# Attention and token mixing on one NeuronCore: output tiles of two batches stored whole, three stores on other queues

## The chip, the core and the metric

The kernel runs on one NeuronCore of a Trainium2 chip. The core has five engines that run side by side, each with its own instruction stream in order: TensorE (PE, matrix products, results into the eight banks of PSUM), VectorE (DVE), ScalarE (ACT), GpSimd (POOL) and SyncE (SP, which here only issues DMAs). DMAs are issued by SyncE, ScalarE or GpSimd, each into its own queue, and carried out by 16 DMA engines that all queues share. Engines wait for each other, and for DMAs that have landed, through semaphores. The metric is device time in microseconds (us) of the whole program.

## The reference

Inputs are fp32: q, k, v of shape (8 batches, 8 heads, 576, 64), p of shape (8, 8, 32, 64), w_q and w_k of 512 x 64 and w_out of 512 x 512. The output is fp32, (8, 576, 512): 9.4 MB.

```python
def _attn_ref(q, k, v, p):
    scale = 1.0 / np.sqrt(q.shape[-1])
    def sm_attn(qq, kk, vv):
        s = scale * np.matmul(qq, kk.transpose(0, 1, 3, 2))
        s = s - np.max(s, axis=-1, keepdims=True)
        a = np.exp(s)
        a = a / (np.sum(a, axis=-1, keepdims=True) + 1e-09)
        return np.matmul(a, vv)
    p_packed = sm_attn(p, k, v)
    return sm_attn(q, p_packed, p_packed)

def _moe_ref(x, w_q, w_k, w_out):     # x: heads side by side, (8, 576, 512)
    wq = x @ w_q
    wk = x @ w_k
    W_tok = scale * np.einsum('bsd,btd->bst', wq, wk)
    mixed = np.einsum('bst,btd->bsd', W_tok, x)
    return np.maximum(mixed, 0.0) @ w_out
```

## The kernel before

The whole program is a list of steps written out by hand, the string ORDER. Each entry is a step with its batch, a part, the engine (`@A` ScalarE, `@V` VectorE, `@P` GpSimd; for a store, none means SyncE) and the PSUM banks (`=0,1`). The loop at the end (L601 to L622) issues the entries in this order, so on every engine, and in every DMA queue, work stands in the order of the string. Semaphore waits are put in where a step reads or overwrites what another step or DMA uses.

For each batch the steps run in this order: loads of k, v and q (LD, all by GpSimd, which casts them to bf16); the first attention (KT, S1, X1, TE, PV, RC, PP, PT); the second attention (QK, QKE, QV, S2, X2, RS, RR, AM, AT, AE); the token mixing with its products WKQ (evacuated by WE), GM (GE), Y (YE), MX and MR (RL, RLF, RLR); and the output products OT with w_out, whose results are copied from PSUM to an fp32 tile in SBUF (OE for two of its four tiles, OEF for one, OEH for a part of one). The batches overlap; the last, batch 7, runs alone at the end.

What the change and the prediction speak of:

- The output of a batch is 4 tiles of 128 x 512 in the buffer `o`, plus a rest of 64 rows that two batches share (`orem`, OEF.b.4). There are NO = 6 `o` buffers of 8 KB per partition, so batch 6 uses the buffer of batch 0 and batch 7 that of batch 1. The partition holds tokens so that its 4 tiles are one run of 8 KB in the output.
- `ST.b.n` (L555) stores tiles 2n and 2n+1 of batch b, 128 rows of 4 KB, 512 KB; `ST.b.4` stores the rest of two batches, 256 KB. `STF.b.t` (L590) stores one tile, 256 KB, and `STH` (L585) a part of batch 7's last one.
- `HOLD.v7` (L567) is a tiny DMA by SyncE that reads the last of v; SyncE issues it once that has landed, and all SyncE's stores stand behind it.
- `OEF.6.2@A` and `OEF.6.3@V` write tiles 2 and 3 of batch 6, `OE.6.0@V` its tiles 0 and 1. `WE.7.0@A` and `WE.7.1@A` copy what `GM.7` multiplies, and stand behind OEF.6.2 on ScalarE. On TensorE, OT.6.0 and OT.6.1 stand between WKQ.7 and GM.7.
- `AM` (L405) is GpSimd's own arithmetic; AM.6.2 is the next after its early stores.

Line 128 is the copy by ScalarE, 132 by VectorE, 441 and 446 the products of WKQ, 467 those of GM, 540 and 578 those of the output.

Of the kernel before, what the change touches and what calls it, by code (L numbers as in the profile page):

```python
# [40 lines left out]
S1.6=4,5,6,7 X1.6.0@A GM.4=0 GE.4@V TE.6.0@V LD.r7 OT.3.1 X1.6.1@A TE.6.1@V Y.4=0,1 OE.3.0@A RS.5.4@V RR.5.4@V  # L41
PV.6.0=4,5 YE.4@A PV.6.1 MX.4.0=6,7 RC.6@V RL.4.0@A PP.6.0@V AM.5.3@P PP.6.1@V PT.6@V MX.4.1=2,3 AM.5.2@P
OT.3.2=0,1 OT.3.3 RL.4.1@A QK.6=4 QKE.6@A QV.6.2@V ST.2.1 S2.6.2=6,7 X2.6.2@A S2.6.3=2,3 ST.3.4 MR.4=4,5
X2.6.3@A OE.3.1@V RLR.4@V KT.7.2@V AT.5.2=6 AE.5.2@A AT.5.3=7 OT.4.0=0,1 OT.4.1 AE.5.3@A WKQ.5.0=4,5 WKQ.5.2
OE.4.0@A ST.1.1@P WKQ.5.1 RS.6.4@V WE.5.2@A RR.6.4@V ST.4.0 ST.0.1@P S1.7=2,3,6,7 X1.7.1@A AM.6.3@V ST.3.0@P
OT.4.2=0,1 GM.5=4 TE.7.1@V OT.4.3 AT.6.3=5 X1.7.0@A TE.7.0@V GE.5@A OE.4.1@A AM.6.2@P AT.6.2=4 ST.2.0 Y.5=6,7
YE.5@A ST.0.0 ST.3.1 PV.7.0=2,3 QV.7.1@V AE.6.3@V QV.7.0@V AE.6.2@A QD.6@P PV.7.1 RC.7@V PP.7.0@V PP.7.1@V
PT.7@V MR.5=0,1 RLR.5@A MX.5.1=6,7 RL.5.1@A MX.5.0=4,5 RL.5.0@V WKQ.6.0=0,1 WKQ.6.1 WKQ.6.2 WE.6.2@A OT.5.4=2
OEF.5.4@A S2.7.1=6,7 ST.5.4 ST.1.0 GM.6=3 GE.6@V X2.7.1@A RS.7.1@V RR.7.1@V S2.7.2=0,1 X2.7.2@A S2.7.0=4,5
QK.7=2 X2.7.0@A RS.7.0@V RR.7.0@V Y.6=6,7 YE.6@A OT.5.2=0,1 MX.6.1=4,5 QKE.7@A MX.6.0=6,7 AM.7.1@P RS.7.2@V  # L50
RR.7.2@V MR.6=2,3 OT.5.3 RLR.6@V RL.6.0@V RL.6.1@A OE.5.1@A ST.4.1 AM.7.0@P OT.5.0=2,3 AM.7.2@P AT.7.0=4
AE.7.0@A AT.7.1=5 AE.7.1@V AT.7.2=6 AE.7.2@V OT.6.2=0,1 OEF.6.2@A QD.7@P WKQ.7.0=4,5 WKQ.7.2 WKQ.7.1 WE.7.0@A
WE.7.1@A STF.6.2 OT.6.0=6,7 OT.6.1 GM.7=0 OE.6.0@V OT.5.1 OE.5.0@V ST.5.1@P GE.7@A Y.7=4,5 OT.6.3 OEF.6.3@V
ST.6.0 STF.6.3 YE.7@A ST.5.0 MR.7=6,7 RLR.7@A MX.7.0=4,5 RLF.7.0.1@A RLF.7.0.0@V MX.7.1=2,3 RLF.7.1.0@A
OT.7.4=0 OEF.7.4@A ST.7.4 RLF.7.1.1@V OT.7.1=6 OEF.7.1@V OT.7.0=7 STF.7.1 OT.7.2=1 OEF.7.0@A OH.7.0=0 STF.7.0
OEF.7.2@A STF.7.2 OEH.7.0@V STH.7.0 OH.7.1=5 OEH.7.1@A STH.7.1@A
"""


# [1 line left out]
def kernel(  # L61
# [27 lines left out]
    P = 128  # L89
# [47 lines left out]
    def halves(x):  # L137
        return slice(x * 64, (x + 1) * 64)
# [79 lines left out]
    T = {}  # L218
# [323 lines left out]
    def orows(b):  # L542
        return out[b].rearrange("(g r) n -> g r n", r=R)[:, 0:8].rearrange("g (y t) n -> g y (t n)", y=2)
# [11 lines left out]
    def ST(b, n, eng, bk):  # L555
        q = {"A": nc.scalar, "P": nc.gpsimd}.get(eng, nc.sync)
        if n == 4:
            dst = out.rearrange("b (g r) n -> (b g) r n", r=R)
            q.dma_start(dst[(b - 1) * GR:(b + 1) * GR, R - 1], T["orem", b // 2])
        elif b in TURN:  # L560
            q.dma_start(orows(b)[:, :, n * 2 * D:(n + 1) * 2 * D],
                        T["o", b][:, 2 * n:2 * n + 2].rearrange("a t n -> a (t n)"))
        else:
            q.dma_start(orows(b)[:, n], T["o", b][halves(n)].rearrange("a t n -> a (t n)"))
# [25 lines left out]
    def STF(b, t, eng, bk):  # L590
# [4 lines left out]
                 PT=PT, QK=QK, QKE=QKE, QD=QD, QV=QV, S2=S2, X2=X2, HA=HA, RS=RS, RR=RR, AM=AM,  # L595
                 AT=AT, AE=AE, WKQ=WKQ, WE=WE, GM=GM, GE=GE, Y=Y, YE=YE, MX=MX, MR=MR, RL=RL, RLF=RLF,
                 RLR=RLR, OT=OT, OE=OE, OEF=OEF, ST=ST, STF=STF,
                 OH=OH, OEH=OEH, STH=STH)

    with tc.manual_schedule():  # L600
        for item in ORDER.split():  # L601
# [9 lines left out]
            elif f[0] == "WARM":  # L611
                n = 128 * int(f[1])
# [38 lines left out]
```

## Time and profile before

| | us |
|---|---|
| median of 3 runs | 104.38 (104.2 to 105.15) |
| the profiled execution | 104.42 |
| its span, first to last instruction | 102.6 |

Below, each digit stands for a fortieth of the span (2.57 us): the share of time that GpSimd was busy, that the 16 DMA engines were busy on the mean, in tenths, and the GB/s that they moved. Loads run to slice 30, stores from there on.

```profile
POOL 5971877993039929724459493649724009300000
...
DMA  1999999999999999999999999999999999997893
GB/s 18 234 230 207 211 215 209 207 210 213 203 212 207 214 209 209 213 210 207 212 210 208 211 212 204 216 211 205 250 250 387 412 413 409 417 388 294 346 370 127
```

The stores as the page counts them (engine whose queue, number, KB of each, median us from issue to landing):

```profile
out_dram<-o SPq DMA_DIRECT2D x9, 512.0 KB, 8.9
...
out_dram<-o POOLq DMA_DIRECT2D x4, 512.0 KB, 9.0
out_dram<-o SPq DMA_DIRECT2D x5, 256.0 KB, 3.0
...
out_dram<-orem SPq DMA_DIRECT2D x3, 256.0 KB, 7.8
```

GpSimd issues ST.1.1, ST.0.1 and ST.3.0 one behind the other after its arithmetic for batch 5, and ST.5.1 near the end. SyncE's order is ST.2.1, ST.3.4, ST.4.0, ST.2.0, ST.0.0, ST.3.1, ST.5.4, ST.1.0, ST.4.1, STF.6.2, ST.6.0, STF.6.3, ST.5.0 and then batch 7. In the views a store by `ST` has line 561 (559 for a rest), one by `STF` line 592, one by `STH` line 588.

### The profile page before, as it was taken

The numbers are of one execution on the slowest core, as the hardware profiler recorded it, in microseconds if no ns is written. First come the engines' busy times: TensorE is split into PE (matmuls) and PEld (weight loads), VectorE is DVE, ScalarE is ACT, GpSimd is POOL, SyncE is SP. The second block draws the span as 40 slices with busy tenths as digits, with TensorE's granted clock in tenths as the row PEclk, the third lists the DMA queues.
The fourth block names the chain that finished last, engine by engine and source line by source line (L and its number), as shares of the span: only waits on it lengthen the run. The fifth ranks groups of instructions, "written<-read, shape, count | busy, mean of one in ns | idle before, by whom it ended". The sixth has DMA issues, their size and how long they took to land.

```text
span 102.6 us, 3594 instructions
## 1 busy us (share of the span) xinstructions
PE 93.2 (91%) x1536; PEld 55.1 (54%) x1536; DVE 73.5 (72%) x140; ACT 65.0 (63%) x111; POOL 53.1 (52%) x83
## 2 busy tenths in 40 slices
PE   5998999998699999999998899989999999999930
PEld 3896555465265633755636557544757565643420
DVE  4164376957979479888697979499999979249420
ACT  1320415178754767849977979887989897726430
POOL 5971877993039929724459493649724009300000
PEclk9999999999999999999999999999999999999997
DMA  1999999999999999999999999999999999997893
GB/s 18 234 230 207 211 215 209 207 210 213 203 212 207 214 209 209 213 210 207 212 210 208 211 212 204 216 211 205 250 250 387 412 413 409 417 388 294 346 370 127
DMA packets 13567, 25.13 MB, mean 245 GB/s; under 512 B 1072, under 2 KB 6448, under 8 KB 13552
## 3 DMA queue, kind: packets, MB, share of 16 engines
q0 software_dynamic: 9936, 17.04, 84.3%
q1 hardware_dynamic: 3056, 7.41, 18.9%
q10 hardware_dynamic: 560, 0.46, 1.9%
q8 instruction: 12, 0.20, 0.7%
q14 instruction: 3, 0.02, 0.1%
HBM read 30.15 MB, written 9.44 MB: 386 GB/s over the span
## 4 chain that ended last, share of the span: by engine, by line
PE 64%; DVE 9%; ACT 8%; DMA 7%; POOL 4%; issue 3%; DVEq 0%; POOLq 0%; ACTq 0%
PE ps L540 26%; PE ps L617 9%; DMA k_sb<-in_k_dram 7%; PE ps L373 5%; PE ps L315 4%; ACT e1T L293 4%; POOL a L405 4%; PE ps L282 3%; PE ps L419 3%; PE ps L446 3%; PE ps L467 3%; DVE rs L394 2%; PE ps L441 2%; PE ps L336 2%; DVE kT L237 2%
## 5 line engine op out<-in xcount | busy, mean ns | idle before, releaser
L540 PE MATMUL ps<-wout,relu 128*128 128x512 bf16 x124 | 30.6, 380 | 0.0
L405 POOL TENSOR_TENSOR a<-e,rr 128x256 bf16<-128x256 f32 (+2 forms) x18 | 19.5, 1099 | 16.4 <-DVE rr L399 6.4
L617 PE MATMUL ps<-o 128*128 128x128 f32 (+3 forms) x76 | 20.0, 410 | 1.2 <-DVE o L135 1.2
L540 PEld LDWEIGHTS <-relu 128*128 128x128 bf16 x124 | 10.7, 98 | 11.7 <-issue 1.1
L128 ACT ACTIVATE o<-ps 128x1024 f32<-128x1024 f32 (+2 forms) x13 | 11.3, 870 | 5.4 <-PE ps L540 5.2
L617 PEld LDWEIGHTS ps<-o 128*128 128x128 f32 x76 | 11.8, 217 | 5.2 <-issue 3.6
L503 ACT ACTIVATE relu<-ps 128x1024 bf16<-128x1024 f32 (+1 forms) x14 | 12.9, 966 | 1.1 <-PE ps L492 1.1
L293 ACT ACTIVATE e1T<-ps 128x576 bf16<-128x576 f32 x16 | 9.8, 655 | 5.2 <-PE ps L282 4.6
L378 ACT ACTIVATE e<-ps 128x256 f32<-128x256 f32 (+2 forms) x19 | 11.2, 622 | 2.5 <-PE ps L373 2.4
L394 DVE TENSOR_REDUCE rs<-e 128x16 f32<-128x512 f32 (+2 forms) x13 | 10.9, 841 | 2.3 <-ACT e L378 2.2
L173 POOL DMA_DIRECT2D v_sb<-in_v_dram x16 | 10.0, 629 | 4.2 <-DMA v_sb<-in_v_dram 1.6
L237 DVE STREAM_TRANSPOSE kT<-k_sb 128x1152 uint32<-128x1152 uint32 (+1 forms) x9 | 11.0, 1226 | 1.4 <-DMA k_sb<-in_k_dram 1.3
L237 DVE STREAM_TRANSPOSE qT<-q_sb 128x1152 uint32<-128x1152 uint32 (+1 forms) x10 | 11.0, 1104 | 0.0
L132 DVE COPY o<-ps 128x1024 f32<-128x1024 f32 (+2 forms) x7 | 6.7, 977 | 5.2 <-PE ps L540 2.7
L237 DVE STREAM_TRANSPOSE e<-e1T 128x288 uint32<-128x288 uint32 x16 | 7.4, 468 | 3.1 <-ACT e1T L293 2.6
L128 ACT ACTIVATE aT<-ps 128x128 bf16<-128x128 f32 (+2 forms) x11 | 5.0, 464 | 5.7 <-PE ps L419 3.3
L128 ACT ACTIVATE wkq<-ps 128x448 bf16<-128x448 f32 (+1 forms) x10 | 7.2, 729 | 1.8 <-PE ps L446 1.7
L315 PE MATMUL ps<-v_sb,e 64*64 64x192 bf16 x288 | 7.5, 245 | 0.8 <-DVE e L237 0.5
L315 PEld LDWEIGHTS <-e 64*64 64x64 bf16 x288 | 5.9, 107 | 2.6 <-DVE e L237 2.0
L373 PEld LDWEIGHTS <-qT 64*128 64x128 bf16 x320 | 5.4, 94 | 2.6 <-DVE qT L237 1.5
L446 PE MATMUL ps<-aT,pqk 128*128 128x256 bf16 (+1 forms) x48 | 6.8, 246 | 0.0
L373 PE MATMUL ps<-ppT,qT 64*128 64x64 bf16 x320 | 6.6, 190 | 0.1
(70 smaller groups left out, 131.5 us busy)
## 6 DMA issues: line engine op xcount, KB each, us to landing
v_sb<-in_v_dram POOLq DMA_DIRECT2D x16, 288.0 KB, 14.5
out_dram<-o SPq DMA_DIRECT2D x9, 512.0 KB, 8.9
k_sb<-in_k_dram POOLq DMA_DIRECT2D x7, 576.0 KB, 14.0
q_sb<-in_q_dram POOLq DMA_DIRECT2D x6, 576.0 KB, 13.5
out_dram<-o POOLq DMA_DIRECT2D x4, 512.0 KB, 9.0
out_dram<-o SPq DMA_DIRECT2D x5, 256.0 KB, 3.0
q_sb<-in_q_dram POOLq DMA_DIRECT2D x4, 288.0 KB, 10.5
out_dram<-orem SPq DMA_DIRECT2D x3, 256.0 KB, 7.8
```

Of the source, the lines that this page charges most:

```text
L128: nc.scalar.activation(o, i, COPY)
L173: nc.gpsimd.dma_start(v_bufs[b % NL][halves(i), 0:7:2], src)
L237: nc.vector.transpose(o, i)
L293: nc.scalar.activation(e1T[:, x], T["s1", b][x].rearrange("a c m -> a m c"), EXP, scale=scale)
L315: nc.tensor.matmul(T["pv", b][halves(cc), i], lhsT, rhs, start=n == 0, stop=n == R - 1, skip_group_check=True)
L373: nc.tensor.matmul(ps[:, y, t - t0, i], lhsT, rhs, start=e == 0, stop=e == 1)
L378: nc.scalar.activation(e2[:, t0:t1].rearrange("a t (i y n) -> a y (t i) n", i=2, y=2), T["s2", b, c].rearrange("a y t i n -> a y (t i) n") ...
L394: nc.vector.tensor_reduce(rs[:, t0 * H:t1 * H], src, axis=AX, op=ADD)
L405: e.tensor_tensor(a2[:, t0:t1].rearrange("a t i (u l) -> a (t i u) l", l=L), e2v(b, c), T["rr", b][:, t0 * H:t1 * H].to_broadcast((P, (t1 ...
L503: nc.scalar.activation(o, i, RELU)
L540: nc.tensor.matmul(ps, lhsT, wout[:, j, :], start=j == 0, stop=j == NJ - 1)
L617: nc.tensor.matmul(bank(int(bk), [w]), warm[:, 0:P], rhs, start=True, stop=True)
```

## The change

ST gets a part 8, the whole tile buffer of a batch in one DMA with rows of 8 KB:

```diff
         if n == 4:
             dst = out.rearrange("b (g r) n -> (b g) r n", r=R)
             q.dma_start(dst[(b - 1) * GR:(b + 1) * GR, R - 1], T["orem", b // 2])
+        elif n == 8:
+            q.dma_start(orows(b), T["o", b].rearrange("a t n -> a (t n)"))
         elif b in TURN:
```

In ORDER these entries move (the others keep their places):

```diff
-X2.6.3@A OE.3.1@V RLR.4@V KT.7.2@V AT.5.2=6
+X2.6.3@A OE.3.1@V RLR.4@V ST.1.8@P KT.7.2@V AT.5.2=6
...
-OE.4.0@A ST.1.1@P WKQ.5.1 RS.6.4@V WE.5.2@A RR.6.4@V ST.4.0 ST.0.1@P S1.7=2,3,6,7 X1.7.1@A AM.6.3@V ST.3.0@P
+OE.4.0@A WKQ.5.1 RS.6.4@V WE.5.2@A RR.6.4@V ST.4.0 ST.3.8@P S1.7=2,3,6,7 X1.7.1@A AM.6.3@V
...
-YE.5@A ST.0.0 ST.3.1 PV.7.0=2,3
+YE.5@A ST.0.0 ST.0.1 PV.7.0=2,3
...
-OEF.5.4@A S2.7.1=6,7 ST.5.4 ST.1.0 GM.6=3
+OEF.5.4@A S2.7.1=6,7 ST.5.4 GM.6=3
...
-OT.5.1 OE.5.0@V ST.5.1@P GE.7@A
+OT.5.1 OE.5.0@V ST.5.1 GE.7@A
```

So GpSimd issues ST.1.8 and ST.3.8, of 1 MB each, in the place of ST.1.1, ST.0.1 and ST.3.0, and no store after them. SyncE's order becomes ST.2.1, ST.3.4, ST.4.0, ST.2.0, ST.0.0, ST.0.1, ST.5.4, ST.4.1, STF.6.2, ST.5.1, ST.6.0, STF.6.3, ST.5.0 and then batch 7.

More of the change, by code (lines that the diff above doesn't have):

```diff
@@ L43 @@
 OT.3.2=0,1 OT.3.3 RL.4.1@A QK.6=4 QKE.6@A QV.6.2@V ST.2.1 S2.6.2=6,7 X2.6.2@A S2.6.3=2,3 ST.3.4 MR.4=4,5
-X2.6.3@A OE.3.1@V RLR.4@V KT.7.2@V AT.5.2=6 AE.5.2@A AT.5.3=7 OT.4.0=0,1 OT.4.1 AE.5.3@A WKQ.5.0=4,5 WKQ.5.2
-OE.4.0@A ST.1.1@P WKQ.5.1 RS.6.4@V WE.5.2@A RR.6.4@V ST.4.0 ST.0.1@P S1.7=2,3,6,7 X1.7.1@A AM.6.3@V ST.3.0@P
-OT.4.2=0,1 GM.5=4 TE.7.1@V OT.4.3 AT.6.3=5 X1.7.0@A TE.7.0@V GE.5@A OE.4.1@A AM.6.2@P AT.6.2=4 ST.2.0 Y.5=6,7
-YE.5@A ST.0.0 ST.3.1 PV.7.0=2,3 QV.7.1@V AE.6.3@V QV.7.0@V AE.6.2@A QD.6@P PV.7.1 RC.7@V PP.7.0@V PP.7.1@V
@@ L48 @@
[L48 to L56, printed above, removed]
+X2.6.3@A OE.3.1@V RLR.4@V ST.1.8@P KT.7.2@V AT.5.2=6 AE.5.2@A AT.5.3=7 OT.4.0=0,1 OT.4.1 AE.5.3@A WKQ.5.0=4,5
@@ new lines @@
+WKQ.5.2 OE.4.0@A WKQ.5.1 RS.6.4@V WE.5.2@A RR.6.4@V ST.4.0 ST.3.8@P S1.7=2,3,6,7 X1.7.1@A AM.6.3@V OT.4.2=0,1
+GM.5=4 TE.7.1@V OT.4.3 AT.6.3=5 X1.7.0@A TE.7.0@V GE.5@A OE.4.1@A AM.6.2@P AT.6.2=4 ST.2.0 Y.5=6,7 YE.5@A
+ST.0.0 ST.0.1 PV.7.0=2,3 QV.7.1@V AE.6.3@V QV.7.0@V AE.6.2@A QD.6@P PV.7.1 RC.7@V PP.7.0@V PP.7.1@V PT.7@V
+MR.5=0,1 RLR.5@A MX.5.1=6,7 RL.5.1@A MX.5.0=4,5 RL.5.0@V WKQ.6.0=0,1 WKQ.6.1 WKQ.6.2 WE.6.2@A OT.5.4=2
+OEF.5.4@A S2.7.1=6,7 ST.5.4 GM.6=3 GE.6@V X2.7.1@A RS.7.1@V RR.7.1@V S2.7.2=0,1 X2.7.2@A S2.7.0=4,5 QK.7=2
@@ new lines @@
+X2.7.0@A RS.7.0@V RR.7.0@V Y.6=6,7 YE.6@A OT.5.2=0,1 MX.6.1=4,5 QKE.7@A MX.6.0=6,7 AM.7.1@P RS.7.2@V RR.7.2@V
+MR.6=2,3 OT.5.3 RLR.6@V RL.6.0@V RL.6.1@A OE.5.1@A ST.4.1 AM.7.0@P OT.5.0=2,3 AM.7.2@P AT.7.0=4 AE.7.0@A
+AT.7.1=5 AE.7.1@V AT.7.2=6 AE.7.2@V OT.6.2=0,1 OEF.6.2@A QD.7@P WKQ.7.0=4,5 WKQ.7.2 WKQ.7.1 WE.7.0@A WE.7.1@A
+STF.6.2 OT.6.0=6,7 OT.6.1 GM.7=0 OE.6.0@V OT.5.1 OE.5.0@V ST.5.1 GE.7@A Y.7=4,5 OT.6.3 OEF.6.3@V ST.6.0
+STF.6.3 YE.7@A ST.5.0 MR.7=6,7 RLR.7@A MX.7.0=4,5 RLF.7.0.1@A RLF.7.0.0@V MX.7.1=2,3 RLF.7.1.0@A OT.7.4=0
@@ L57 @@
+OEF.7.4@A ST.7.4 RLF.7.1.1@V OT.7.1=6 OEF.7.1@V OT.7.0=7 STF.7.1 OT.7.2=1 OEF.7.0@A OH.7.0=0 STF.7.0 OEF.7.2@A
+STF.7.2 OEH.7.0@V STH.7.0 OH.7.1=5 OEH.7.1@A STH.7.1@A
 """
```

## The prediction

> **What bounds the kernel now.** I read the page's shares first, then the chain of waits over the last 18 us.
>
> ```profile
> PE 93.2 (91%) x1536; PEld 55.1 (54%) x1536; DVE 73.5 (72%) x140; ACT 65.0 (63%) x111; POOL 53.1 (52%) x83
> ```
> ```profile
> 88.57 0.12 PE ps L441 x4
> ...
> 89.35 1.73 PE ps L540 x8
> 91.08 0.29 PE ps L467 x10
> 91.37 0.86 PE ps L540 x4
> ...
> 94.03 3.63 PE ps L540 x16
> 97.66 0.67 PE ps L578 x4
> ...
> 98.40 0.56 DVE o L132
> ```
>
> The columns are start, length and what ran. TensorE (PE) has hardly a gap: L441 is the last projection of batch 7 (WKQ.7), L540 and L578 are the products with w_out, and L467 is GM.7, from which all the rest of batch 7 follows in one line. After the copy OEH.7.0 at 98.40 only the last stores are left. So a change here costs time if it moves GM.7 and gains only if it shortens that line.
>
> Stores are on no link of that chain, but they are near it. A store matters in one way before the end: until it has landed, the o buffer that it reads can't be written again. There are 6 buffers for 8 batches, so batch 6 writes into batch 0's buffer and batch 7 into batch 1's. These are the first steps of ScalarE that do so, from its timeline:
>
> ```profile
> 88.60 0.60 ACT L128 ACTIVATE o<-ps 128x512 f32<-128x512 f32 x1 [0.55 <-PE ps L540]
> 89.10 0.97 ACT L128 ACTIVATE wkq<-ps 128x448 bf16<-128x448 f32 x2
> 91.41 0.28 ACT L128 ACTIVATE g<-ps 128x128 bf16<-128x128 f32 x1 [1.34 <-PE ps L467]
> ```
>
> The row at 88.60 is OEF.6.2@A, which writes tile 2 of o buffer 0, the tile that ST.0.1 reads. The row behind it is WE.7.0@A and WE.7.1@A, the operands of GM.7. Now ST.0.1 is GpSimd's second store; start and issue-to-landing (last column) are:
>
> ```profile
> 72.51 0.62 POOL L561 DMA_DIRECT2D out_dram<-o  x1
> out_dram<-o POOLq DMA_DIRECT2D x1, 512.0 KB, 9.7
> ```
>
> It lands at 72.51 + 9.7 = 82.2, which is 6.4 us ahead of OEF.6.2. The wait exists and is hidden.
>
> **The change part by part.**
>
> *ST.0.1 moves to SyncE, behind ST.0.0.* That is the sixth store of SyncE's queue, the place that ST.3.1 had. From SyncE's timeline and the issues, for ST.0.0 and then ST.3.1:
>
> ```profile
> 78.68 1.21 SPq L561 DMA_DIRECT2D out_dram<-o  x1
> out_dram<-o SPq DMA_DIRECT2D x1, 512.0 KB, 10.4
> 79.94 0.60 SPq L561 DMA_DIRECT2D out_dram<-o  x1
> out_dram<-o SPq DMA_DIRECT2D x1, 512.0 KB, 10.4
> ```
>
> They landed at 89.1 and 90.3. So even with nothing else changed, ST.0.1 in that place would land 1.7 us after OEF.6.2 wants its tile. (The wait goes by tiles and not by the whole buffer: OEF.6.2 began at 88.60, before ST.0.0, which reads tiles 0 and 1, had landed.)
>
> *GpSimd stores batches 1 and 3 whole.* Its early stores grow from three of 512 KB to two of 1 MB: from 1.5 to 2.0 MB. Whether the extra 512 KB lies ahead of ST.0.1 is read from the DMA queues (q0 is GpSimd's, q1 SyncE's; packets, MB, share of 16 engines) at 76 to 80, 80 to 84 and 84 to 88 us:
>
> ```profile
> q0 software_dynamic: 428, 1.40, 101.5%
> q1 hardware_dynamic: 50, 0.02, 2.1%
> ...
> q1 hardware_dynamic: 423, 1.30, 81.2%
> q0 software_dynamic: 111, 0.36, 22.4%
> ...
> q1 hardware_dynamic: 478, 1.62, 100.6%
> ```
>
> GpSimd's stores were issued first; its queue is emptied first and is gone by 84, six us before ST.3.1 landed, and SyncE's queue hardly moves until 80. With 0.52 MB more it would be gone by about 85.3, still long before ST.0.1's bytes. The engines are full (100.6%) and move 1.62 MB in 4 us, 0.405 MB per us. So 0.524 MB ahead costs 1.3 us, and the two SyncE stores above, 1.2 us apart in landing, say the same. ST.0.1 lands at 90.3 + 1.3 = 91.6, and ST.0.0 at 89.1 + 1.3 = 90.4.
>
> *The row length.* A row of 8 KB is in no store of this trace. Below: the 2 KB rows that fill the queue at 95.5 to 96 us take more time per byte than the 4 KB rows above:
>
> ```profile
> q1 hardware_dynamic: 92, 0.19, 102.3%
> ```
>
> That is 0.19 MB in 8.2 us of engine time, 23.2 KB per us, against 1.62 MB in 64.4 us, 25.2 KB per us. If doubling the row again gave as much again (8%), the 2.1 MB of GpSimd would take 0.4 us less of their 5.2 us. Above: the largest packets of the page, the instruction queue's,
>
> ```profile
> q8 instruction: 12, 0.20, 0.7%
> ```
>
> run at 0.20 MB in 0.7% of 16 x 102.6 us, 17 KB per us; at that rate the two stores would take 2.4 us more. They are reads of another kind, and the nearest row is the 4 KB store, so I take no difference.
>
> A fixed cost per DMA, of which one fewer now stands ahead of ST.0.1, isn't seen between them: the two 512 KB stores above landed 1.2 us apart, which their bytes alone take. The Trainium skill (DMA: Bandwidth & Descriptors, Anatomy of one DMA — SWDGE (gpsimd) path) gives a DMA some 2 us beside its bytes and asks for DMAs of 1 MiB; paid one after the other, that would make the sum 2 us less here (B below), and this trace disagrees by the 1.2 us.
>
> *What the wait costs.* OEF.6.2 goes from 88.60 to 91.6: 3.0 us later. Queued behind it on ScalarE are WE.7.0 and WE.7.1 (their end goes from 89.10 + 0.97 = 90.07 to 93.07), then GE.7, YE.7 and the rest of batch 7; on SyncE STF.6.2 waits for the same tile, and with it ST.5.1, ST.6.0 and all later stores. On TensorE the eight products OT.6.0 and OT.6.1 stand between WKQ.7 and GM.7 (89.35 to 91.08) and need neither; they cover 91.08 - 90.07 = 1.0 us. The rest, 3.0 - 1.0 = 2.0 us, is idle time of TensorE before GM.7, whose work is in a fixed order, so nothing moves into the gap. Small corrections cancel: four of GM.7's ten products need only WE.7.0 (0.1 us earlier), and the signal of the landing has to reach ScalarE (0.1 us later).
>
> After GM.7 the line is dependent to its end and moves by the same 2.0 us. One thing can give some back. VectorE's copies
>
> ```profile
> 91.12 3.05 DVE L132 COPY o<-ps 128x1024 f32<-128x1024 f32 x3 [2.74 <-PE ps L540]
> 94.08 1.28 DVE L505 TENSOR_SCALAR relu<-ps 128x512 bf16<-128x512 f32 x2
> ```
>
> stand packed in front of two of the four RLF.7 steps; the first (OE.6.0) stays at about 91.1, as ST.0.0 lands at 90.4, and the others move. The sixteen products at 94.03 take 3.63 us, 0.23 each, where eight at 89.35 take 0.216 each, so at most 0.2 us comes back. I count nothing.
>
> *The rest has one answer.* ST.1.0 and ST.3.1 leave SyncE, and ST.5.1 comes from GpSimd. No later step writes batch 3's or 5's buffer, and ST.1.8, now first on GpSimd, lands long before OEF.7.1 writes batch 1's. On GpSimd the rows are:
>
> ```profile
> 71.56 1.23 DVE L132 COPY o<-ps 128x1024 f32<-128x1024 f32 x1
> 71.84 1.89 POOL L561 DMA_DIRECT2D out_dram<-o  x3
> 76.36 1.58 POOL L405 TENSOR_TENSOR a<-e,rr 128x256 bf16<-128x256 f32 x1 [2.63 <-DVE rr L399]
> ```
>
> ST.3.8 now needs OE.3.1@V (the first row), over at 72.79, 0.3 us after GpSimd reaches it; it delays only itself, since GpSimd is idle 2.63 us before AM.6.2. Two issues instead of three, at 0.63 each or up to twice that for twice the bytes, fit in the same cover (2.5 us at most against 1.89); without it 0.6 us would be on AM.6.2. STF.6.2 and ST.6.0 on SyncE:
>
> ```profile
> 89.23 0.54 SPq L592 DMA_DIRECT2D out_dram<-o  x1
> 92.37 0.54 SPq L561 DMA_DIRECT2D out_dram<-o  x1
> ```
>
> Issuing ST.5.1 between them costs SyncE another 0.54 us; in the new order STF.6.2 goes out at about 92.2 and ST.6.0 at 93.3, and nobody waits for either.
>
> At the end, SyncE's stores from STF.6.2 on are 3.4 MB (ST.5.1 with them), 8.4 us at 0.405 MB per us. Issued from 92.2, with their first bytes some 1.5 us later, they end near 102.1. The last one, issued at 98.99 now and with this row,
>
> ```profile
> 98.99 0.54 SPq L588 DMA_DIRECT2D out_dram<-o  x1
> out_dram<-o SPq DMA_DIRECT2D x1, 192.0 KB, 2.5
> ```
>
> would be issued at 101.0 and land at 103.5, so it isn't held up by a backlog.
>
> Sum: 3.0 - 1.0 = +2.0 us. The profiled execution took 104.42 us with a span of 102.6 (1.8 us around it); the median of the three times is 104.38, within 0.04. So 106.4 us.
>
> **The rivals.**
>
> *A. Not slower: the 512 KB more on GpSimd's queue delay nothing on SyncE's.* The place is the landing of ST.0.1. If the engines served SyncE's queue beside GpSimd's, as in 80 to 84 us where q1 has 81% and q0 22%, or gained 0.4 us by longer rows, the landing would stay near 90.3. Then OEF.6.2 is 1.7 us late, 1.0 of it covered: 104.4 + 0.7 = 105.1 us. It decides from a landing at 90.6: earlier, the loss is under 1.04 us, which is 1%, about what a measurement of this kernel can tell from no change. Against it: the queue's emptying by 84 whatever the share in between.
>
> *B. The merging itself pays.* The last store, 192 KB, took 2.5 us to land, of which its bytes at 0.405 MB per us are 0.5: 2.0 us belong to no byte. If GpSimd's queue paid them between its stores, two in place of three would land ST.0.1 at 91.6 - 2.0 = 89.6; the cover of 1.0 us takes the rest, and the time is 104.4 us. Against it stand the two landings 1.2 us apart.
>
> *C. The idle time costs clock.* TensorE's granted clock after its last product (OH.7.1, over by 98.53), over the two stretches 98.53 to 101.14 and 101.20 to the end:
>
> ```profile
> 98.53:101.14 2.61, 0.00 (x0) 0.00 (x0) 0.43 (x1) 0.28 (x1) 0.00 (x0) 1.00 0.94 339
> 101.20:102.60 1.40, 0.00 (x0) 0.00 (x0) 0.00 (x0) 0.00 (x0) 0.00 (x0) 0.50 0.01 2
> ```
>
> After 2.6 us without work the clock (third number from the end) is halved. The new gap, from 91.08 to 93.1, is 0.6 us shorter than that, so I expect full clock. If the gap grows or is counted otherwise, the products behind it run at half clock. How long isn't shown: between the 1.4 us seen above and all of the 7.2 us left (91.08 to 98.32); midway, some 4 us, of which half is lost, gives 106.4 + 2 = 108.4. The Trainium skill (TensorE: Matmul & The Clock Gate, Part 1: The HAM clock gate) puts the gate's free-running window at 3.4 us, by which a gap of 2.0 us doesn't close it; the row here, closed after 2.6 us, shows that less than 3.4 us after the last product can be enough.
>
> *D. Rows of 8 KB go at 17 KB per us*: landing 2.4 us later, 108.8.
>
> **How the numbers follow.** Forecast, 106.4 (105.6 to 107.2 by its own terms, some 0.8 us on the landing): 0.70. A: 0.12. B: 0.05. C: 0.09. D: 0.04. The range goes from 104.9, which takes in A, to 107.9, a landing 1.5 us later than worked out, and leaves out B, C and D, together 0.18. Slower by over 1% (above 105.4): the forecast, C and D, 0.83. Within 1%: A and most of B, 0.14. Faster by over 1%: 0.03, a rest of B, since no link of the chain gets shorter.
>
> **What would show it.** Right: ST.0.1 lands near 91.6; OEF.6.2 begins then, and the idle time before it is ended by a DMA of out_dram; TensorE shows one new gap of about 2 us before L467; from there each row is shifted alike; OE.6.0 stays at 91.1; the clock stays at 1.00 until the last product. Wrong: OEF.6.2 at 88.6, a landing before 90, AM.6.2 late behind GpSimd's issues, last stores taking well over 2.5 us, or a gap at another place.

## The result and the profile after

| | before | after |
|---|---|---|
| median, us | 104.38 (104.12 to 105.15, 5 runs) | 106.25 (105.83 to 106.47, 5 runs) |
| ratio after to before | | 1.016, 95% interval 1.0132 to 1.0187 |
| profiled execution, us (span) | 104.42 (102.6) | 106.47 (104.7) |

The changed kernel is 1.9 us slower; 106.4 was forecast. In its code line 561 is the whole store, 563 an `ST` with rows of 4 KB, 594 an `STF`, 590 an `STH`. ScalarE's timeline in the changed kernel, at the place that the prediction named:

```profile
87.67 0.60 ACT L128 ACTIVATE aT<-ps 128x512 bf16<-128x512 bf16 x1
91.25 0.60 ACT L128 ACTIVATE o<-ps 128x512 f32<-128x512 f32 x1 [2.98 <-DMA out_dram<-o]
91.74 0.97 ACT L128 ACTIVATE wkq<-ps 128x448 bf16<-128x448 f32 x2
```

The first row is the copy that stands in front of OEF.6.2 (the aT copy). OEF.6.2 begins at 91.25 instead of 88.60, after 2.98 us in which ScalarE did nothing and which a store ended. Of these, 0.55 us were there before, for the products that OEF.6.2 copies; the store adds some 2.4. ST.0.1, in the views of SyncE's timeline and of the issues, is

```profile
79.86 0.60 SPq L563 DMA_DIRECT2D out_dram<-o  x1
out_dram<-o SPq DMA_DIRECT2D x1, 512.0 KB, 11.3
```

issued at 79.86 and landed at 91.2. TensorE's timeline shows the gap that comes of it, between the last output products in front of GM.7 and GM.7 itself (L467), with 0.16 us more between its first four products and the other six, as each part waits for its own WE.7:

```profile
89.40 1.89 PE L540 MATMUL ps<-wout,relu 128*128 128x512 bf16 x7
92.33 0.28 PE L467 MATMUL ps<-wkq,a 128*128 128x64 bf16 x4 [1.04 <-ACT wkq L128]
92.77 0.34 PE L467 MATMUL ps<-wkq,a 128*128 128x64 bf16 x6 [0.16 <-ACT wkq L128]
```

The chain of waits runs through the store now, and after GM.7 through the same links as before:

```profile
79.86 11.30 DMA out_dram<-o
...
91.25 0.07 ACT o L128
...
91.74 0.98 ACT wkq L128 x2
...
92.77 0.34 PE ps L467 x6
93.10 0.86 PE ps L540 x4
...
100.14 0.56 DVE o L132
```

The six products end at 93.10 where GM.7 ended at 91.37: 1.73 us later. The last copy starts at 100.14 where it started at 98.40: 1.74 us later. So nothing is lost or regained in between. Some 0.2 us of it is no part of the wait, as the aT copy above stood at 87.46 before; that leaves 1.5. What remains stands behind it, in the last store:

```profile
out_dram<-o SPq DMA_DIRECT2D x1, 192.0 KB, 3.0
```

It took 3.0 us where it took 2.5. Before, ScalarE's store landed last, 0.2 us behind SyncE's, so only 0.3 of these 0.5 us make the program longer: 0.2 + 1.5 + 0.3 is 2.0, of the 2.05 us between the two profiled executions.

### The profile page after: what moved, and what is told of

Same layout as the page of the kernel before. It is cut to its first block, busy times and chain, and to the rows that moved or that the text cites. A ratio compares the mean times of both kernels' runs of the same rounds, so it can differ in the third digit from the quotient of the medians.

```text
span 104.7 us, 3575 instructions
## 1 busy us (share of the span) xinstructions
PE 92.9 (89%) x1521; PEld 55.9 (53%) x1536; DVE 73.7 (70%) x140; ACT 65.0 (62%) x111; POOL 52.0 (50%) x81
## 4 chain that ended last, share of the span: by engine, by line
PE 54%; DVE 11%; DMA 11%; ACT 11%; issue 5%; POOL 4%; DVEq 0%; ACTq 0%; POOLq 0%
PE ps L619 17%; PE ps L540 17%; DMA out_dram<-o 11%; ACT e1T L293 5%; PE ps L373 4%; POOL a L405 4%; PE ps L315 3%; PE ps L419 2%; DVE rs L394 2%; DVE e L237 2%; PE ps L282 2%; ACT wkq L128 2%; PE ps L336 2%; PE ps L446 1%; PE ps L467 1%
## 5 line engine op out<-in xcount | busy, mean ns | idle before, releaser
L540 PE MATMUL ps<-wout,relu 128*128 128x512 bf16 x112 | 29.5, 380 | 0.9 <-issue 0.3
L619 PE MATMUL ps<-o 128*128 128x128 f32 (+3 forms) x76 | 20.8, 426 | 1.2 <-DVE o L135 1.2
L619 PEld LDWEIGHTS ps<-o 128*128 128x128 f32 x76 | 12.7, 233 | 5.3 <-issue 3.6
L446 PE MATMUL ps<-aT,pqk 128*128 128x256 bf16 (+1 forms) x48 | 6.8, 246 | 0.0
## 6 DMA issues: line engine op xcount, KB each, us to landing
q_sb<-in_q_dram POOLq DMA_DIRECT2D x4, 288.0 KB, 10.3
```

The source lines that it names most:

```text
L540: nc.tensor.matmul(ps, lhsT, wout[:, j, :], start=j == 0, stop=j == NJ - 1)
L619: nc.tensor.matmul(bank(int(bk), [w]), warm[:, 0:P], rhs, start=True, stop=True)
```

## The experiments

Two theories were put against each other. The wait theory: the loss is OEF.6.2 waiting for ST.0.1's landing. The rival: the loss is DMA work itself (rows of 8 KB, more bytes on GpSimd's queue, ST.5.1 among the last stores), and would be there without the wait. The table gives the median, the 95% interval of the ratio to the kernel before, run on the same chip, and four readings of each profiled execution: where ST.0.1 landed (issue plus the time to landing), where OEF.6.2 and GM.7 began (us), and how long SyncE's last store took. Executions differ by some tenths of a us from the start; that of e2 is the slowest of its kernel (105.36), and the steps read here come about 1.2 us late in it. The diffs show the entries around what moves, without the rest of their lines.

| | median us | ratio | ST.0.1 landed | OEF.6.2 | GM.7 | last store |
|---|---|---|---|---|---|---|
| before | 104.38 | | 82.2 | 88.60 | 90.92 | 2.5 |
| changed | 106.25 | 1.0132 to 1.0187 | 91.2 | 91.25 | 92.33 | 3.0 |
| e1_swap_only | 104.68 | 0.9987 to 1.0023 | 89.9 | 89.96 | 91.45 | 2.5 |
| e2_first | 104.53 | 0.9979 to 1.0021 | 85.8 | 89.76 | 92.08 | 2.5 |
| e3_rows4k | 106.59 | 1.0166 to 1.0228 | 91.5 | 91.58 | 92.66 | 3.1 |
| e4_other_buffer | 104.44 | 0.9975 to 1.0026 | 91.2 | 88.48 | 90.79 | 2.5 |
| e5_st51_pool | 105.90 | 1.0107 to 1.0172 | 91.2 | 91.24 | 92.32 | 2.5 |
| e6_later | 109.20 | 1.0419 to 1.0493 | 93.3 | 93.36 | 94.44 | 2.5 |
| e7_batch0_whole | 104.42 | 0.9987 to 1.0026 | 85.6 | 88.85 | 91.16 | 2.5 |
| e8_fifth | 105.16 | 1.0047 to 1.0115 | 89.8 | 89.87 | 91.23 | 3.0 |
| e9_fifth_st51_pool | 104.78 | 1.0005 to 1.0047 | 89.7 | 89.79 | 91.26 | 2.5 |
| e10_st51_ahead | 105.65 | 1.0097 to 1.0148 | 90.9 | 91.00 | 92.08 | 2.5 |
| e11_changed_again | 106.38 | 1.0158 to 1.021 | 91.1 | 91.15 | 92.36 | 2.9 |

**The wait alone taken away (e4_other_buffer).** Batch 6 writes into batch 2's buffer; no DMA changes.

```diff
-        T[key, b] = T[key][b % bufs]
+        T[key, b] = T[key][2 if (key, b) == ("o", 6) else b % bufs]
```

> The changed kernel with batch 6's output in the buffer of batch 2 instead of batch 0; every DMA in its place, size and queue as changed. Wait theory: OEF.6.2 now needs ST.2.1, landed at 84.9, so it starts at 88.8, GM.7 follows the products before it without a gap, 104.4 to 104.7 us. Rival (DMA work): 106.2 us. If the store tail counts for itself, 104.8 or more, with a last store over 2.7 us.

The whole loss is gone: 104.44. ScalarE's timeline:

```profile
88.48 0.60 ACT L128 ACTIVATE o<-ps 128x512 f32<-128x512 f32 x1 [0.55 <-PE ps L540]
88.97 0.97 ACT L128 ACTIVATE wkq<-ps 128x448 bf16<-128x448 f32 x2
```

ST.0.1 lands at 91.2 as in the changed kernel, but nobody waits for it. The last store is back at 2.5 us too, so the longer tail needs the wait; the stores' number and place alone don't make it. The rival falls here.

**ST.0.1 earlier (e2_first, e7_batch0_whole).** The first puts ST.0.1 at the head of SyncE's stores; the second has GpSimd store batch 0 whole instead of batch 3.

```diff
 e2_first
-ST.0.0 ST.0.1 PV.7.0
+ST.0.0 PV.7.0
-QV.6.2@V ST.2.1
+QV.6.2@V ST.0.1 ST.2.1
 e7_batch0_whole
-ST.4.0 ST.3.8@P
+ST.4.0 ST.0.8@P
-ST.0.0 ST.0.1 PV.7.0
+ST.3.0 ST.3.1 PV.7.0
```

> The changed kernel with ST.0.1 first among SyncE's stores, ahead of ST.2.1; rows and the bytes of each queue as changed. Wait theory: ST.0.1 lands near 85, no ScalarE wait on a DMA, 104.4 us, less up to 0.3 if the longer rows help. Rival (DMA work): 106.2 us, as changed.

> The changed kernel with batch 0 stored whole by GpSimd's second DMA instead of batch 3, whose two stores take the places of batch 0's on SyncE. Queues, bytes, rows as changed. Wait theory: batch 0 lands near 85, no wait, 104.4 us; no gain over the kernel before, as its chain held no wait for a store. If the longer rows or the earlier landings gain something: under 104.2. Rival (DMA work): 106.2 us.

Both are at the time of the kernel before, 104.53 and 104.42. Whole stores with rows of 8 KB on GpSimd's queue cost nothing, and gain nothing that can be measured.

**The move alone (e1_swap_only).** In the kernel before, ST.0.1 and ST.3.1 change places.

```diff
-ST.4.0 ST.0.1@P S1.7
+ST.4.0 ST.3.1@P S1.7
-ST.0.0 ST.3.1 PV.7.0
+ST.0.0 ST.0.1 PV.7.0
```

> The kernel before with one exchange: ST.0.1 goes to SyncE's sixth place and ST.3.1 to GpSimd's second; all rows of 4 KB, the bytes of each queue as before. Wait theory (the loss is OEF.6.2 waiting for the landing of ST.0.1): it lands at 90.3, ScalarE idles 1.7 us on a DMA of out_dram before OEF.6.2, 1.0 of it covered, 105.1 us. Rival (the loss is DMA work: 8 KB rows, 2 MB on GpSimd's queue, three stores more at the end): as before, 104.4 us.

The wait theory expected 105.1, and 104.68 was measured, no difference from the kernel before. That is what the rival expected, so by its time this run does not speak against the rival; e4 does. (Of the stores, only ST.5.1 goes later on SyncE in the changed kernel, not three.) ScalarE's and TensorE's timelines:

```profile
88.00 0.60 ACT L128 ACTIVATE aT<-ps 128x512 bf16<-128x512 bf16 x1
89.96 0.60 ACT L128 ACTIVATE o<-ps 128x512 f32<-128x512 f32 x1 [1.36 <-PE ps L446]
```
```profile
89.73 1.89 PE L540 MATMUL ps<-wout,relu 128*128 128x512 bf16 x7
91.45 0.45 PE L467 MATMUL ps<-wkq,a 128*128 128x64 bf16 x10
```

The row names TensorE as what ended the wait, but OEF.6.2 needs nothing of L446, and ST.0.1 landed at 89.88, 0.08 before it began: it was the store. In the kernel before, OEF.6.2 began 1.14 us after the aT copy in front of it (88.60 - 87.46), which is 89.14 here. So it was 0.8 us late and not 1.7: the landing came 0.4 earlier than ST.3.1's in the profile of before, and this execution's copies ran 0.5 later. 0.8 us is inside the cover of 1.0, and TensorE shows no gap: the wait is there, and too short to cost anything.

**The row length (e3_rows4k).** The same bytes at the same places in four stores with rows of 4 KB, so the run has two DMAs more as well.

```diff
-ST.1.8@P
+ST.1.0@P ST.1.1@P
-ST.3.8@P
+ST.3.0@P ST.3.1@P
```

> The changed kernel with ST.1.8 and ST.3.8 each cut into two stores with rows of 4 KB on the same queue at the same place. Wait theory: rows matter only through the landing of ST.0.1, which comes 0.2 to 0.4 us later than the 91.2 of the changed kernel, 106.4 to 106.7 us. Rival (8 KB rows cost): the landing gets earlier and the time falls towards 105.

106.59, with the landing and OEF.6.2 0.3 us later than in the changed kernel. As times the two intervals overlap, so the 0.3 us rests on one profile of each, and it holds the row length and a cost per DMA together. The DMA view from 78 to 79 us agrees, first of the kernel before (rows of 4 KB), then of the changed one (rows of 8 KB):

```profile
q0 software_dynamic: 112, 0.40, 99.2%
```
```profile
q0 software_dynamic: 61, 0.42, 102.1%
```

That is 0.40 MB in 15.9 us of engine time, 25.2 KB per us, and 0.42 MB in 16.3, 25.7 KB per us: the longer row is some 2% faster, as far as two digits tell, and not slower.

**Where ST.5.1 stands (e5_st51_pool, e10_st51_ahead).** In the changed kernel it waits behind STF.6.2, which waits with OEF.6.2. The first puts it back on GpSimd, the second ahead of STF.6.2 on SyncE.

```diff
 e5_st51_pool
-OE.5.0@V ST.5.1 GE.7@A
+OE.5.0@V ST.5.1@P GE.7@A
 e10_st51_ahead
-OE.5.0@V ST.5.1 GE.7@A
+OE.5.0@V GE.7@A
-OE.5.1@A ST.4.1 AM.7.0@P
+OE.5.1@A ST.4.1 ST.5.1 AM.7.0@P
```

> The changed kernel with ST.5.1 back on GpSimd, so that it no longer stands behind STF.6.2, which waits with OEF.6.2. The wait stays (landing near 91.2, ScalarE idle 3 us). If the held-back stores add 0.5 us at the end (last store 3.0 us in the changed kernel against 2.5 in the one before): the last store takes 2.5 us again and the time falls by 0.4 to 0.5, to 105.8 us. If they add nothing: 106.2 us.

> The changed kernel with ST.5.1 still on SyncE but ahead of STF.6.2, so that it is issued before the wait. Held-back stores: the last store takes 2.5 us, the time is that of e5_st51_pool, 105.7 to 105.9 us, and the queue that ST.5.1 is on doesn't matter. If only the queue matters: 106.2 us with a last store of 3.0.

105.90 and 105.65, both with a last store of 2.5 us. Beside the changed kernel run again on the same chip (e11, 1.0158 to 1.021), e10 (1.0097 to 1.0148) is clear of it; the interval of e5 overlaps that of the changed kernel. What happens is seen in the stretches 90 to 92 and 92 to 94 us; the last two numbers of a row are the DMA engines' busy share and GB/s. The kernel before, the changed kernel, then e10:

```profile
90.00:92.00 2.00, 2.00 (x19) 0.98 (x17) 0.88 (x1) 0.35 (x2) 0.00 (x0) 1.00 1.01 410
92.00:94.00 2.00, 1.98 (x18) 0.69 (x16) 2.00 (x3) 0.79 (x3) 0.00 (x0) 1.00 0.66 260
```
```profile
90.00:92.00 2.00, 1.29 (x6) 0.49 (x5) 0.67 (x1) 0.75 (x2) 0.00 (x0) 1.00 0.40 160
92.00:94.00 2.00, 1.51 (x18) 0.75 (x17) 0.56 (x1) 0.99 (x3) 0.00 (x0) 1.00 0.56 203
```
```profile
90.00:92.00 2.00, 1.43 (x7) 0.56 (x6) 0.53 (x1) 1.00 (x3) 0.00 (x0) 1.00 0.87 353
92.00:94.00 2.00, 1.76 (x19) 0.87 (x19) 0.94 (x2) 0.80 (x4) 0.00 (x0) 1.00 0.65 241
```

With SyncE's queue held the DMA engines run dry, and 512 KB that could have gone in the gap go later. In e10's profile GM.7 also begins 0.28 us earlier than in e11's (92.08, 92.36), so not all of its gain is the store's place.

**One place earlier (e8_fifth, e9_fifth_st51_pool).** ST.0.1 and ST.0.0 change places in the changed kernel; e9 has ST.5.1 back on GpSimd as well.

```diff
-ST.0.0 ST.0.1 PV.7.0
+ST.0.1 ST.0.0 PV.7.0
```

> The changed kernel with ST.0.1 and ST.0.0 exchanged on SyncE, so ST.0.1 is fifth. Wait theory: it lands 1.2 us earlier than in the changed kernel, at 90.0, 1.2 late for OEF.6.2 by the times there, 1.0 of it covered: 104.5 to 104.8 us, 1.4 to 1.7 less than the changed kernel; OE.6.0 then waits for ST.0.0 at 91.2, when it is due anyway. Rival (DMA work): 106.2 us.

> The kernel of e8_fifth (ST.0.1 fifth on SyncE, where the wait only used up the cover) with ST.5.1 back on GpSimd. If the 0.8 us that e8_fifth lost are held-back stores at the end: the wait before OEF.6.2 stays near 1.5 us, the last store takes 2.5 us instead of 3.0, and the time is 104.4 to 104.6 us. If they are the wait itself, uncovered in part: 105.1 us, as e8_fifth.

e8 took 105.16, above what was expected of it. TensorE has no gap (the output products from 89.51, GM.7 right behind them at 91.23), so the wait of 1.0 us is all covered, and yet 0.8 us are lost: the last store takes 3.0 us. With ST.5.1 out of the way (e9) it takes 2.5 and the time is 104.78, above the 104.4 to 104.6 that held-back stores alone would give and below the 105.1 of the wait. The intervals of e8 and e9 touch at 1.0047, and e9 is a little above the kernel before (1.0005 to 1.0047), so most, not provably all, of e8's loss is the held queue.

**Two places later (e6_later).** ST.0.1 stands behind ST.5.4 and ST.4.1.

```diff
-ST.0.0 ST.0.1 PV.7.0
+ST.0.0 PV.7.0
-OE.5.1@A ST.4.1 AM.7.0@P
+OE.5.1@A ST.4.1 ST.0.1 AM.7.0@P
```

> The changed kernel with ST.0.1 two places later on SyncE, behind ST.5.4 and ST.4.1 (0.75 MB). Wait theory: landing 1.9 us later, near 93.0; TensorE idle some 3 us before GM.7 with two thirds of a us inside it for the first products; every us counts in full, 106.25 + 1.9 = 108.1 us. If an idle stretch of about 3 us halves the granted clock, as 2.6 us after the last product did in the kernel before: 109 to 111 us, and the clock shows 0.50 after the gap. Rival (DMA work): 106.2 us, as the DMAs are the same in another order.

109.2 us, inside the case with a halved clock. The stretches before GM.7, behind it and to the end (the third number from the end is the granted clock):

```profile
91.50:94.40 2.90, 0.10 (x1) 0.00 (x0) 1.23 (x1) 1.04 (x3) 0.00 (x0) 1.00 0.06 25
95.70:99.00 3.30, 3.30 (x18) 0.80 (x16) 1.66 (x2) 0.64 (x2) 0.00 (x0) 0.50 0.86 336
99.10:103.00 3.90, 3.90 (x22) 1.76 (x19) 2.11 (x4) 2.36 (x6) 0.00 (x0) 1.00 0.67 257
```

The landing at 93.3 is 2.1 us later than in the changed kernel. From OEF.6.2 to the last copy's start it takes 103.67 - 93.36 = 10.3 us, where the changed kernel takes 100.14 - 91.25 = 8.9: the half clock cost 1.4 us. The last store takes 0.5 us less. 2.1 + 1.4 - 0.5 = 3.0, and the medians differ by 2.95.

**The changed kernel again (e11_changed_again).**

> The changed kernel itself, beside the two above on the same chip: 106.2 us, the last store 3.0 us, the landing of ST.0.1 between 91.0 and 91.4.

106.38. Its profiled execution holds a control that nobody planned: TensorE's clock was halved early on, in this stretch of e11,

```profile
29.20:32.50 3.30, 3.30 (x77) 2.71 (x69) 2.10 (x6) 1.47 (x3) 1.95 (x3) 0.50 1.17 210
```

and ScalarE's timeline runs 1.2 us late at the aT copy:

```profile
88.90 0.60 ACT L128 ACTIVATE aT<-ps 128x512 bf16<-128x512 bf16 x1
91.15 0.60 ACT L128 ACTIVATE o<-ps 128x512 f32<-128x512 f32 x1 [1.65 <-DMA out_dram<-o]
```

OEF.6.2 begins at 91.15 all the same and the execution takes 106.19 us. The wait is shorter by what the engines lost: 1.2 us lost ahead of the landing cost nothing. That is about all that can be lost there, as TensorE comes to GM.7 without a gap in this execution (at 92.36).

## Why the prediction was right, by its steps

*The bound and the wait.* Right. OEF.6.2's hidden wait becomes one of some 2.4 us (2.98 idle in all), GM.7 is where TensorE's gap opens (1.04 and 0.16 us, where one of about 2 us was foreseen), and e4 shows that this wait is the cause of all of it.

*The landing, 91.6 worked out, 91.2 measured.* Right in kind. The bytes are priced right: between e1 and e5, which differ in ST.1.0 going ahead on GpSimd's queue and in its row length, the landing moves by 91.2 - 89.9 = 1.3 us, and the median by 105.90 - 104.68 = 1.2 (1.4 by the ratios, as the two ran on different chips). What was too dear is the move by itself: 0.7 us by the sum, 0.1 (within the noise) in e1. It was taken from one profile's landing, and landings in this place and the times of the engines shift against each other by some tenths from one execution to the next. The 8 KB rows, put at nothing, brought back about 0.3 of the bound of 0.4, by one profile of each.

*The cover, 1.0 us.* Right for TensorE: in e1 and e8, where OEF.6.2 is about 0.8 and 1.0 us late, there is no gap. In the changed kernel OEF.6.2 is 2.65 us late and GM.7 ends 1.73 late, a cover of 0.9.

*"So it isn't held up by a backlog."* Wrong. That step let SyncE's stores from STF.6.2 on go without a break from 93.7 and end near 102.1, ahead of the last one's landing at 103.5. The bytes did begin at about 93.0 (from 92 to 93 us the DMA engines are 5% busy, from 93 to 96 they are full). But STF.6.3 still has to wait 2.1 us for its tile, and from 96 to 97 us the engines are 39% busy; from 97 to 102 they are 98% busy, so there is a backlog, and the last store takes 3.0 us, one of the prediction's own signs of being wrong. The prediction named STF.6.2 and ST.5.1 as held back and said that nobody waits for either; nobody does, but the bytes are then at the end. e5 took 0.35 us less than the changed kernel, within the noise, and e10 0.7 less, of which 0.28 is an earlier GM.7. So the sum of 2.0 us came out, by luck, through two misses against each other: the wait is worth some 1.5 us (GM.7's end, less the 0.2 that were there before), the tail some 0.3 to 0.5.

*The corrections counted at nothing.* Right: VectorE's copies made room but the line from GM.7 to the last copy was shifted by the same 1.7 us. GpSimd's two issues took 0.67 and 0.64 us, as for half the bytes, and ST.3.8 waited 0.58 us for OE.3.1, which delayed nothing else.

*The rivals.* A had the place right: without the extra half MB (e1) the time is that of before. That the bytes lie ahead of ST.0.1 is shown by the landings of GpSimd's stores, at most 85.3 in the changed kernel, as worked out. B is refuted by e3: with four stores in place of two, ST.0.1 lands 0.3 us later and not 4. (e2 and e7 show only that the merged stores gain no time where nobody waits for them.) C didn't happen here, with TensorE idle for 1.04 us and then 0.16 by the timeline, and did in e6. D is refuted by the row rates.

## What to carry to other kernels

A store that reads a buffer to be written again has a due time, as a load has: give it its place in the queues by that time, and count every byte that any queue has ahead of it. When an engine waits for such a store, look at the queue that waits with it: stores held behind the wait leave the DMA engines dry and come back at the end, even where the wait itself is covered by other work. Whether such a loss is the wait or the transfers is told apart by one run in which the writer takes a buffer that has long been free.

## What the runs showed of the hardware

After an idle stretch of TensorE of 2.84 us in the middle of work (e6) its granted clock was halved, but not at once. All six executions of e6 have a mean clock of 0.976 to 0.984, where the five of the changed kernel have 0.989 to 1.000. In e6's stretches around the change

```profile
95.40:95.60 0.20, 0.20 (x3) 0.10 (x1) 0.00 (x0) 0.13 (x1) 0.00 (x0) 1.00 1.00 369
95.62:95.90 0.28, 0.28 (x3) 0.00 (x0) 0.00 (x0) 0.00 (x0) 0.00 (x0) 0.50 1.14 432
```

the clock falls at 95.6, over a us after the products had begun again at 94.44, and is whole again from 99.0, some 3.4 us later. The Trainium skill (TensorE: Matmul & The Clock Gate, Part 1: The HAM clock gate) has a window of 3.4 us that runs free of the program; the length of the half clock agrees with that. The Trainium skill's figure there for closing, one idle window of 3.4 us, doesn't agree with a gap of 2.84 us.

The length of one gap isn't all that decides. The changed kernel kept its clock through a gap of 1.04 us, but in e11 the clock was halved from about 29.2 on with no gap longer than 0.97 in the 7 us ahead of it. In the two stretches just before, TensorE was busy about half of the time:

```profile
26.00:28.00 2.00, 1.03 (x12) 0.55 (x10) 1.55 (x5) 1.56 (x2) 0.00 (x0) 1.00 1.20 203
28.00:29.10 1.10, 0.60 (x12) 0.16 (x12) 1.10 (x2) 0.00 (x0) 0.00 (x0) 1.00 1.15 214
```

In the kernel before, the second of these stretches is busy for 1.09 of its 1.10 us, and the clock stays whole. Where the limit lies was not tried.
